# Output product of a slot-based expert layer: float32 in the two halves of TensorE's rows in place of float32r operands in two parts

## Chip, cores and metric

The kernel runs on one core of one Trainium2 chip. The metric is the device time of one execution in microseconds (us), lower is better. All times of instructions come from one profiled execution.

## Reference

An input of 8 x 2496 rows of 256 values goes through a two-dimensional Fourier transform, of which the real part is kept. The result `x` (19968 rows) passes a soft mixture of experts with 32 slots (8 experts of 4 slots):

```python
logits = x @ phi                                   # 19968 x 32
d = exp(logits - logits.max(0)); d /= d.sum(0)     # over rows
slot_out[e] = relu((d.T @ x)[e] @ w1[e]) @ w2[e]   # 32 x 256 in all
c = exp(logits - logits.max(1)); c /= c.sum(1)     # over slots
return c @ slot_out                                # 19968 x 256
```

The change concerns the last line: every row of the output is a sum of 32 products, float32.

## The kernel before

The 8 batches are worked on as four pairs p. For each pair the rows are loaded and folded (`part_a`), transformed and multiplied with phi in several small products (`part_z`, `part_t`, `part_b`, `part_c`), and the exponentials over rows give the slot inputs (`part_e`, `part_d`, `part_u`). `part_m`, `part_l` and `part_v` merge the pairs and run the two expert layers; their result is `so` in PSUM, one copy of the slots in each of four groups of 32 partitions. `part_r` sums the four groups with one product by the table `sel2` (tile `sorep`, L515), so that each group of 32 partitions holds the whole 32 x 256 `slot_out`, and writes it as the moving operand `rh`.

`part_s(p)` transposes the logits of a pair (tile `cT`, L534, three PSUM tiles), copies them to `c` with ScalarE (L539), and normalises them over the slots in two halves of 20 places: maximum on VectorE (L548), subtraction on GpSimd (L549), exponential on ScalarE (L550), sum and reciprocal on VectorE (L551 to L553), product on GpSimd (L554). A place is 128 rows of output with 32 weights each, so `c` is 128 partitions x 40 places x 32 slots.

The output is then made in 20 tiles (p, b): four pairs, five tiles each, eight places in a tile. Of each tile:

- `part_q` has split `c` in two parts, both float32r: ScalarE casts it (L560), and VectorE subtracts the cast from it (L561). The tile `hl` holds for each place 32 values of the first part and 32 of the second.
- `part_o` transposes two places at a time (four transposes, `lT`, L574), so that 128 partitions hold place, part and slot. ScalarE copies the four to `lTs` (L575).
- For each of the four couples i of places, two products (j = 0, 1) of 128 x 128 by 128 x 512 accumulate in one PSUM bank `po` (L581). `rh[0]` holds the cast of `slot_out` and `rh[1]` what the cast left over, each with zeros where a place meets the other's columns.
- ScalarE copies even i to the output tile and VectorE odd i (L585). SyncE writes the tile to memory when it is full (L590, L592).

PSUM banks: even i take turns on two (`ps`), odd i on three (`ps3`), and `lT` and `cT` share two (`p1`). Six output tiles can be in flight (`RING`), three `lTs` (`et`). The parts are written in the order of the string `ORDER`, and the framework's scheduler then sets the order of the instructions on each engine; every engine works in that order. The float32 products of the earlier stages give a `tile_position`, a place in the array: L246, L378, L477 and L497 use a quarter of its columns, L337 and L355 a half. L231, L281, L299, L300, L534 use the whole.

Of the kernel before, what the change touches and what calls it, by code (L numbers as in the profile page):

```python
# [5 lines left out]

F32 = mybir.dt.float32
F32R = mybir.dt.float32r
AF = mybir.ActivationFunctionType
ALU = mybir.AluOpType  # L10
AX = mybir.AxisListType
# [5 lines left out]
D = 256  # L17
NSLOT = 32
# [7 lines left out]
LA = 0  # L26
LD = '0 00 1 01 p 02 03 04 10 11 12 2 13 14 3'.split()
LT = 4
CT = ['sa', 'lt', 'lt', 'lt']
HT = ['se', 'zs']  # L30
RH = 0
LATE = 'zs'
SEB = 2
DE = 2
GP = 3
FIRST = [0, 1]
# [3 lines left out]
    "a00 z00 a01 z01 a02 z02 t00 a10 z10 b00 a11 z11 c00 c01 e00 e01 d00 a12 z12 t10 a20 z20 a21 z21 "  # L40
    "a22 z22 d01 b10 c10 e10 u00 a30 z30 d10 t20 c11 e11 b20 d11 c20 c21 a31 z31 "
    "e20 a32 z32 t30 e21 u10 b30 d20 c30 w00 d21 c31 u20 e30 e31 d30 d31 "
    "u30 m00 l00 s00 l10 q00 s10 v00 v10 r00 o00 q01 o01 q10 o02 o03 "
    "o04 o10 s20 q11 o11 q20 o12 o13 q21 o14 s30 o20 o21 q30 o22 o23 "
    "q31 o24 o30 o31 o32 o33 o34"
).split()


# [1 line left out]
def _tables():  # L50
    j = np.arange(128)
# [9 lines left out]
    c = np.arange(NKC)  # L61
# [7 lines left out]
    def block(t):  # L69
        return np.kron(eye, t)  # L70

    half = np.where(kc == 0, 0.5, 1.0)[:, None]
    ta = np.concatenate([cj[1:], co[:1]])
    g = np.arange(128) // NSLOT
    s = np.arange(128) % NSLOT
# [24 lines left out]
        ("psum", (g[:, None] // 2 * NSLOT + s[:, None]) == np.arange(64)),  # L100
        ("sel", np.arange(6)[:, None] + 6 * (np.arange(256) // 128) == np.tile(s, 2) // GS),
        ("sel2", s[:, None] == s[None]),
    ]
    out, where = [], {}
    for group in (zero, first, third, second, late):
        width = sum(t.shape[1] for _, t in group)
        arr = np.zeros((128, width), np.float32)
        o = 0
# [8 lines left out]
def _build(nc, tc, xh, phih, w1h, w2h, cins, where, out, out0):  # L117
    from contextlib import ExitStack, nullcontext

    v, sc, pe = nc.vector, nc.scalar, nc.tensor  # L120
    ctx = ExitStack()
    with ctx:
        cp = ctx.enter_context(tc.tile_pool(name="cp", bufs=1))
        sb = ctx.enter_context(tc.tile_pool(name="sb", bufs=1))
# [4 lines left out]
        def ring(name):  # L129
            return sb.tile([128, 8, D], F32, name=name, tag="ring", bufs=RING)  # L130
# [7 lines left out]
        def et(shape, name, dt=F32):  # L138
            return sb.tile(shape, dt, name=name, tag="et", bufs=3)

        def bufs_(tag):
            return {"zs": 2, "sa": 2, "se": SEB, "lt": LT}[tag]

        def bank(name, dt=F32):
            return pp.tile([128, 512], dt, name=name, tag="ps")
# [4 lines left out]
        def bank1(name, dt=F32):  # L150
            return p1.tile([128, 512], dt, name=name, tag="p1")
# [25 lines left out]
        def C(name):  # L177
            i, o, r, w = where[name]
            return cs[i][:r, o : o + w]

        ident = C("ident")
# [3 lines left out]
        ps = bank("psphi")  # L185
# [23 lines left out]
        zs, zt, o1, dpm, esb, dsb = {}, {}, {}, {}, {}, {}  # L209
# [217 lines left out]
        anchor = {}  # L427
# [41 lines left out]
        rh = []  # L469
# [34 lines left out]

        def part_r():
            so = sos_[0]
            for j in range(2):
                rh.append(sb.tile([128, 2, D], F32R, name=f"rh{j}", tag="d", bufs=2))
                nc.gpsimd.memset(rh[j].bitcast(F32), 0.0)
            v.tensor_copy(identr, ident)  # L510
            sos = sb.tile([128, D], F32, name="sos", tag="dpm", bufs=2)
            ps = bank("sorep")
            sc.copy(sos[:, :128], so[:, :128])
            v.tensor_copy(sos[:, 128:], so[:, 128:D])
            pe.matmul(ps[:, :D], C("sel2"), sos, start=True, stop=True)  # L515
            half = [slice(0, 64), slice(64, 128)]
            sc.copy(rh[0][half[0], 0, :], ps[half[0], :D])
            (v.tensor_copy if RH else sc.copy)(rh[0][half[1], 1, :], ps[half[1], :D])
            for k, r in enumerate(half):
                v.tensor_tensor(rh[1][r, k, :], ps[r, :D], rh[0][r, k, :].bitcast(F32), op=ALU.subtract)  # L520

        identr = sb.tile([128, 128], F32R, name="identr", tag="mex2", bufs=1)


        hl, cq = {}, {}

        def part_s(p):
            L = lt[p]
# [24 lines left out]
                v.reciprocal(m[:, 1], m[:, 1])  # L553
                e2.tensor_tensor(c, c, m[:, 1].unsqueeze(2).to_broadcast([128, 20, NSLOT]), op=ALU.mult)  # L554

        def part_q(p, i):
            c = cq[p][:, 20 * i : 20 * i + 20]
            e3 = nc.gpsimd if GP & 4 else v
            t = sb.tile([128, 20, 2, NSLOT], F32R, name=f"hl{p}_{i}", tag=HT[i], bufs=bufs_(HT[i]))
            sc.copy(t[:, :, 0], c)  # L560
            e3.tensor_tensor(t[:, :, 1], c, t[:, :, 0].bitcast(F32), op=ALU.subtract)  # L561
            hl[p, i] = t


        n_ev = [0]

        def part_o(p, b):
            ps = bank1(f"lT{p}_{b}", F32R)
            lT = et([128, 4, 128], f"lTs{p}_{b}", F32R)
            with tc.issue_after(anchor["v1"]) if LA and p == 0 else nullcontext():  # L570
              for i in range(4):
                k0 = 8 * b + 2 * i
                src = hl[p, k0 // 20][:, k0 % 20 : k0 % 20 + 2].rearrange("p k h s -> p (k h s)")
                pe.transpose(ps[:, i * 128 : i * 128 + 128], src, identr)  # L574
            sc.copy(lT, ps.rearrange("p (i n) -> p i n", i=4))  # L575
            ot = ring(f"o{p}_{b}")
            done = 0
            for i in range(4):
                po = (bank, bank3)[i % 2](f"po{p}_{b}_{i}")
                for j in range(2):  # L580
                    pe.matmul(  # L581
                        po, lT[:, i, :], rh[j].rearrange("p k d -> p (k d)"), start=j == 0, stop=j == 1,
                    )
                np_ = 64 if b == 4 and i == 3 else 128
                (v.tensor_copy if n_ev[0] % 2 else sc.copy)(  # L585
                    ot[:np_, 2 * i : 2 * i + 2, :].rearrange("p k d -> p (k d)"), po[:np_]
                )
                n_ev[0] += 1
                if b == 4 and i == 3:
                    nc.sync.dma_start(out0[p].rearrange("p (r d) -> p r d", d=D), ot[:64, 6:8])  # L590
                elif i == 3 or (b == 4 and i == 2) or ((p, b) == (0, 0) and i in FIRST):
                    nc.sync.dma_start(  # L592
                        out[p, :, (8 * b + done) * D : (8 * b + 2 * i + 2) * D].rearrange("p (r d) -> p r d", d=D),
                        ot[:, done : 2 * i + 2],
                    )
                    done = 2 * i + 2

        def after(f, *a):
            at_ = {0: None, 1: anchor.get("u"), 2: anchor.get("l")}[CAFTER]
            if at_ is None:  # L600
                return f(*a)
            with tc.issue_after(at_):
                return f(*a)
# [2 lines left out]
            "a": part_a, "z": part_z, "t": lambda p, _: part_t(p), "b": lambda p, _: part_b(p), "c": part_c,  # L606
            "e": part_e, "d": part_d, "u": lambda p, _: part_u(p), "w": lambda *_: load_w(),
            "m": lambda *_: part_m(), "l": lambda i, _: part_l(i), "v": lambda i, _: part_v(i),
            "r": lambda *_: part_r(), "s": lambda p, _: after(part_s, p), "q": lambda p, i: after(part_q, p, i), "o": part_o,
        }  # L610
        for what in ORDER:
            parts[what[0]](int(what[1]), int(what[2]))
# [50 lines left out]
```

## Time and profile before

| what | value |
|---|---|
| median of 3 runs | 196.1 us (195.84 to 196.13) |
| profiled execution | 195.98 us, span 194.2 us |
| TensorE busy | 170.9 us, 88% of the span |
| VectorE, ScalarE busy | 131.2 and 120.5 us |
| GpSimd busy | 24.6 us |
| written to memory | 20.45 MB |
| first product of the last stage | at 136.67 us |
| last copy of the last stage | at 184.83 us |

In the rows of the profile a group is given as line, engine, operation, out<-in, sizes and count, then busy us and mean ns of one, then the idle time ahead and what ended it. PE is TensorE's product, PEld its weight load, DVE VectorE, ACT ScalarE, POOL GpSimd, SPq the queue of SyncE. A piece of the chain of waits has start, length, engine and line.

### The profile page before, as it was taken

The numbers are of one execution on the slowest core, as the hardware profiler recorded it, in microseconds if no ns is written. First come the engines' busy times: TensorE is split into PE (matmuls) and PEld (weight loads), VectorE is DVE, ScalarE is ACT, GpSimd is POOL, SyncE is SP. The second block draws the span as 40 slices with busy tenths as digits, with TensorE's granted clock in tenths as the row PEclk, the third lists the DMA queues.
The fourth block names the chain that finished last, engine by engine and source line by source line (L and its number), as shares of the span: only waits on it lengthen the run. The fifth ranks groups of instructions, "written<-read, shape, count | busy, mean of one in ns | idle before, by whom it ended". The sixth has DMA issues, their size and how long they took to land.

```text
span 194.2 us, 4324 instructions
## 1 busy us (share of the span) xinstructions
PE 170.9 (88%) x1722; PEld 124.2 (64%) x1722; DVE 131.2 (68%) x238; ACT 120.5 (62%) x261; POOL 24.6 (13%) x27
## 2 busy tenths in 40 slices
PE   0489799899999989999998999999999999989900
PEld 0375496576776857577854877357788867768600
DVE  0599869999995971712456734994777888967600
ACT  2133686578954584775843827745868988997610
POOL 0000000000000000000000203576003157400000
PEclk9999999999999999999999999999999999999985
DMA  5999999999970699403940889970299999799996
GB/s 180 404 427 412 420 416 423 417 419 422 408 250 0 191 395 427 176 0 102 273 169 3 295 277 361 414 286 1 74 417 366 412 410 379 305 425 368 418 432 216
DMA packets 10707, 59.17 MB, mean 305 GB/s; under 512 B 1344, under 2 KB 1728, under 8 KB 5696
## 3 DMA queue, kind: packets, MB, share of 16 engines
q1 hardware_dynamic: 10688, 58.91, 77.1%
q8 instruction: 13, 0.21, 0.5%
q14 instruction: 6, 0.05, 0.1%
HBM read 38.46 MB, written 20.45 MB: 303 GB/s over the span
## 4 chain that ended last, share of the span: by engine, by line
PE 78%; DVE 7%; ACT 5%; DMA 2%; POOL 2%; issue 2%; SPq 0%; ACTq 0%; DVEq 0%; POOLq 0%
PE po L581 17%; PE pt L231 10%; PE z L246 8%; PE e L337 7%; PE d L355 5%; PE a L281 5%; PE u L378 4%; PE h L477 4%; PE so L497 4%; PE cT L534 3%; DMA x<-xh 2%; PE lp L299 2%; PE lm L300 2%; PE lT L574 2%; POOL c L549 2%; PE zt L267 2%
## 5 line engine op out<-in xcount | busy, mean ns | idle before, releaser
L581 PE MATMUL po<-rh,lTs 128*128 128x512 f32 x160 | 42.4, 405 | 1.5 <-ACT lTs L575 0.7
L581 PEld LDWEIGHTS po<-rh,lTs 128*128 128x128 f32 x160 | 28.1, 188 | 8.6 <-ACT o L585 1.8
L231 PE MATMUL pt<-cs,eo 128*128 128x128 f32 x160 | 25.7, 295 | 7.9 <-DVE eo L226 7.7
L585 DVE COPY o<-po 128x512 f32<-128x512 f32 (+1 forms) x40 | 26.9, 686 | 7.9 <-PE po L581 7.0
L232 ACT COPY et<-pt 128x512 f32<-128x512 f32 x40 | 22.8, 587 | 14.0 <-PE pt L231 13.9
L231 PEld LDWEIGHTS pt<-cs,eo 128*128 128x128 f32 x160 | 19.2, 150 | 14.6 <-DVE eo L226 7.7
L585 ACT COPY o<-po 128x512 f32<-128x512 f32 x40 | 23.2, 595 | 7.3 <-PE po L581 7.1
L224 DVE TENSOR_TENSOR x<-x 128x1024 f32<-128x1024 f32 x16 | 19.3, 1214 | 3.2 <-DMA x<-xh 3.2
L246 PE MATMUL z<-et,wphi 128*32 128x256 f32 (+1 forms) x288 | 16.8, 368 | 2.3 <-ACT et L232 2.3
L322 ACT ACTIVATE d<-lt,nm 120x128 f32<-120x128 f32 x44 | 13.7, 391 | 3.6 <-DVE nm L319 3.6
L549 POOL TENSOR_TENSOR c<-c,cm 128x640 f32<-128x640 f32 x8 | 11.8, 1487 | 27.1 <-DVE cm L548 26.0
L246 PEld LDWEIGHTS z<-et,wphi 128*32 128x32 f32 x288 | 8.1, 114 | 9.2 <-ACT et L232 3.8
L337 PE MATMUL e<-cs,dpm 120*64 120x120 f32 x176 | 13.9, 273 | 0.0
L226 DVE TENSOR_TENSOR eo<-x 128x512 f32<-128x512 f32 x20 | 13.7, 683 | 0.3
L227 DVE TENSOR_TENSOR eo<-x 128x512 f32<-128x512 f32 x20 | 13.6, 679 | 0.0
L337 PEld LDWEIGHTS e<-cs,dpm 120*64 120x64 f32 x176 | 11.4, 136 | 2.4 <-issue 1.8
L281 PE MATMUL a<-cs,zt 128*120 128x128 f32 x88 | 11.8, 279 | 1.0 <-DVE lt L304 0.9
L254 ACT COPY zs<-z 128x512 f32<-128x512 f32 (+1 forms) x12 | 6.2, 514 | 10.4 <-PE z L246 10.4
L554 POOL TENSOR_TENSOR c<-c,cm 128x640 f32<-128x640 f32 x8 | 11.0, 1391 | 10.0 <-DVE cm L553 5.5
L575 ACT CAST lTs<-lT 128x512 fp32r<-128x512 f32 x20 | 11.5, 599 | 0.9 <-PE lT L574 0.9
L281 PEld LDWEIGHTS a<-cs,zt 128*120 128x120 f32 x88 | 10.4, 183 | 2.1 <-DVE lt L304 1.1
L378 PE MATMUL u<-eo,ds 128*32 128x129 f32 x320 | 11.5, 275 | 0.1
(99 smaller groups left out, 242.5 us busy)
## 6 DMA issues: line engine op xcount, KB each, us to landing
x<-xh SPq DMA_DIRECT2D x16, 1024.0 KB, 11.9
out<-o SPq DMA_DIRECT2D x15, 1024.0 KB, 4.9
w<-w1h SPq DMA_DIRECT2D x6, 1024.0 KB, 8.4
w<-w2h SPq DMA_DIRECT2D x12, 512.0 KB, 6.2
x<-xh SPq DMA_DIRECT2D x4, 896.0 KB, 12.4
out<-o SPq DMA_DIRECT2D x4, 768.0 KB, 6.3
w<-w1h SPq DMA_DIRECT2D x4, 512.0 KB, 5.1
w<-w2h SPq DMA_DIRECT2D x2, 1024.0 KB, 7.0
```

Of the source, the lines that this page charges most:

```text
L224: v.tensor_tensor(x[:, 0:4], x[:, 0:4], x[:, 4:8], op=ALU.add)
L226: v.tensor_tensor(e[:, :, 0:128], x[:, 0:4, 0:128], x[:, 0:4, 128:256], op=ALU.add)
L231: pe.transpose(b[:, g * 128 : g * 128 + 128], e[:, g, k * 128 : k * 128 + 128], ident)
L232: sc.copy(tr[k][:, :, :, qi, :], b.rearrange("p (g h a) -> p g h a", g=4, h=2))
L246: pe.matmul(z[32 * g : 32 * g + 32, o : o + n], wphi[:, w, :], tr[k][:, g].rearrange("p h q a -> p (h q a)"), start=w != 0, stop=w != 1, t ...
L281: pe.matmul(ps[:120, i * 128 : i * 128 + 128], zt[p][:, GS * g : GS * g + GS].rearrange("p s h c -> p (s h c)"), C("wa"), start=True, stop ...
L322: sc.activation(d[:, g], L[:, g], AF.Exp, bias=nm[:, g : g + 1], scale=1.0)
L337: pe.matmul(ps[64 * k : 64 * k + 64, 120 * i : 120 * i + 120], dpm[p, hf][:, k, 3 * j + i, :], C(name), start=True, stop=True, tile_positi ...
L378: last = pe.matmul(ub[32 * g : 32 * g + 32, 0:129], dsb[p][:, k, c, :], e[:, 0:129] if k == 0 else e[:, 127:256], start=cc == 0, stop=cc == 9,
L549: e1.tensor_tensor(c, c, m[:, 0].unsqueeze(2).to_broadcast([128, 20, NSLOT]), op=ALU.subtract)
L581: pe.matmul(po, lT[:, i, :], rh[j].rearrange("p k d -> p (k d)"), start=j == 0, stop=j == 1,)
L585: (v.tensor_copy if n_ev[0] % 2 else sc.copy)(ot[:np_, 2 * i : 2 * i + 2, :].rearrange("p k d -> p (k d)"), po[:np_])
```

## The change

The two-part operands go. `part_q` with its cast and its subtraction is removed, and so are `identr`, `rh[1]` and the two memsets. `c` itself, in float32, is transposed: one transpose takes four places (128 partitions of place and slot), so a tile has two transposes instead of four, and `lTs` has 256 columns instead of 512.

A couple i of places then stands in 64 partitions: even i in 0 to 63, odd i in 64 to 127. Each couple takes one float32 product with 64 rows, 128 columns and 512 moving columns, at the place (0, 0) or (64, 0) of the array. `rh` is one float32 tile, 128 x 2 x 256: in each group of 32 partitions one of the two blocks of 256 columns holds `slot_out` and the other zeros. ScalarE writes the one block as the product of `sorep` with a column of the new table `turn`, VectorE the other. `turn` is 1 where the group number is even, in its first column, or odd, in its second. Two places that follow each other are issued together and then copied out, as before by ScalarE for even i and VectorE for odd i.

```diff
-            for j in range(2):
-                rh.append(sb.tile([128, 2, D], F32R, name=f"rh{j}", tag="d", bufs=2))
-                nc.gpsimd.memset(rh[j].bitcast(F32), 0.0)
-            v.tensor_copy(identr, ident)
+            rh.append(sb.tile([128, 2, D], F32, name="rh", tag="d", bufs=2))
...
-            sc.copy(rh[0][half[0], 0, :], ps[half[0], :D])
-            (v.tensor_copy if RH else sc.copy)(rh[0][half[1], 1, :], ps[half[1], :D])
-            for k, r in enumerate(half):
-                v.tensor_tensor(rh[1][r, k, :], ps[r, :D], rh[0][r, k, :].bitcast(F32), op=ALU.subtract)
+            sc.activation(rh[0][:, 0], ps[:, :D], AF.Copy, scale=C("turn")[:, 0:1])
+            v.tensor_scalar(rh[0][:, 1], ps[:, :D], C("turn")[:, 1:2], None, op0=ALU.mult)
...
-        def part_q(p, i):
-            c = cq[p][:, 20 * i : 20 * i + 20]
-            e3 = nc.gpsimd if GP & 4 else v
-            t = sb.tile([128, 20, 2, NSLOT], F32R, name=f"hl{p}_{i}", tag=HT[i], bufs=bufs_(HT[i]))
-            sc.copy(t[:, :, 0], c)
-            e3.tensor_tensor(t[:, :, 1], c, t[:, :, 0].bitcast(F32), op=ALU.subtract)
-            hl[p, i] = t
...
-              for i in range(4):
-                k0 = 8 * b + 2 * i
-                src = hl[p, k0 // 20][:, k0 % 20 : k0 % 20 + 2].rearrange("p k h s -> p (k h s)")
-                pe.transpose(ps[:, i * 128 : i * 128 + 128], src, identr)
-            sc.copy(lT, ps.rearrange("p (i n) -> p i n", i=4))
+            for t in range(2):
+                k0 = 8 * b + 4 * t
+                pe.transpose(
+                    ps[:, t * 128 : t * 128 + 128], cq[p][:, k0 : k0 + 4].rearrange("p k s -> p (k s)"), ident
+                )
+            sc.copy(lT, ps[:, :256].rearrange("p (i n) -> p i n", i=2))
...
             for i in range(4):
-                po = (bank, bank3)[i % 2](f"po{p}_{b}_{i}")
-                for j in range(2):
-                    pe.matmul(
-                        po, lT[:, i, :], rh[j].rearrange("p k d -> p (k d)"), start=j == 0, stop=j == 1,
-                    )
+                pos.append((bank, bank3)[i % 2](f"po{p}_{b}_{i}"))
+                rows = slice(64 * (i % 2), 64 * (i % 2) + 64)
+                pe.matmul(
+                    pos[i], lT[rows, i // 2], rh[0][rows].rearrange("p k d -> p (k d)"),
+                    start=True, stop=True, tile_position=(64 * (i % 2), 0),
+                )
+                if i % 2 == 0:
+                    continue
+                part_ev(p, b, i - 1, pos[i - 1], ot)
+                part_ev(p, b, i, pos[i], ot)
```

The scheduler's order changes with it. On TensorE, from the transposes of pair 1's first tile to those of pair 2's logits (in `po_2_1` the tile is b = 2 and the couple i = 1; the last number is the buffer's), there stands before:

```order
L574 MATMUL lT_0_1819<-identr,hl_0_1740 128x128 x4
L581 MATMUL po_2_3_1763<-rh_1671,lTs_2_1744 128x512
L581 MATMUL po_2_3_1763<-rh_1673,lTs_2_1744 128x512
L581 MATMUL po_2_0_1751<-rh_1671,lTs_2_1744 128x512
L581 MATMUL po_2_0_1751<-rh_1673,lTs_2_1744 128x512
L581 MATMUL po_3_1_1780<-rh_1671,lTs_3_1769 128x512
L581 MATMUL po_3_1_1780<-rh_1673,lTs_3_1769 128x512
L581 MATMUL po_2_2_1759<-rh_1671,lTs_2_1744 128x512
L581 MATMUL po_2_2_1759<-rh_1673,lTs_2_1744 128x512
L534 MATMUL cT_0_1845<-cs_70,lt_943 128x120 x4
```

And after, to the second group of those transposes:

```order
L555 MATMUL lT_0_1773<-cs_70,c_1568 128x128 x2
L565 MATMUL po_2_1_1723<-rh,lTs_2_1716 128x512
L565 MATMUL po_2_3_1729<-rh,lTs_2_1716 128x512
L565 MATMUL po_2_0_1721<-rh,lTs_2_1716 128x512
L565 MATMUL po_3_1_1742<-rh,lTs_3_1735 128x512
L565 MATMUL po_2_2_1727<-rh,lTs_2_1716 128x512
L525 MATMUL cT_0_1793<-cs_70,lt_942 128x120 x4
L565 MATMUL po_3_3_1748<-rh,lTs_3_1735 128x512
L565 MATMUL po_4_1_1761<-rh,lTs_4_1754 128x512
L565 MATMUL po_3_0_1740<-rh,lTs_3_1735 128x512
L565 MATMUL po_4_3_1767<-rh,lTs_4_1754 128x512
L565 MATMUL po_3_2_1746<-rh,lTs_3_1735 128x512
```

Couples with odd i, which are in the lower half of the rows now, stand two in a row at the head of both stretches, and each stretch has two even and three odd ones.

On ScalarE, around pair 2's exponentials (`c_1844` before, `c_1792` after, is pair 2's weights), there stands before:

```order
L539 COPY c_1844<-cT_2_1857 128x40x8
L585 COPY o_4_1800<-po_4_0_1801 128x512
L585 COPY o_4_1800<-po_4_2_1809 128x512
L575 COPY lTs_1_1882<-lT_1_1881 128x512
L575 COPY lTs_2_1910<-lT_2_1909 128x512
L585 COPY o_0_1826<-po_0_0_1827 128x512
L550 ACTIVATE c_1844<-c_1844 128x640
```

And after:

```order
L530 COPY c_1792<-cT_2_1805 128x40x8
L579 COPY o_4_1758<-po_4_0_1759 128x512
L541 ACTIVATE c_1792<-c_1792 128x640
L579 COPY o_4_1758<-po_4_2_1765 128x512
L558 COPY lTs_1_1827<-lT_1_1826 128x256
L558 COPY lTs_2_1846<-lT_2_1845 128x256
L541 ACTIVATE c_1792<-c_1792 128x640
L579 COPY o_0_1778<-po_0_0_1779 128x512
```

The first exponential has moved from behind five copies to behind one. Around the end of `so`, two of pair 0's five groups of `lT` have moved into the products of `so` (L497), and the other three stand between `so` and `sorep`; before, two stood between them, two behind `sorep` and one in the product.

## Prediction before the run

> **What bounds the kernel now.** I read the page's groups first, then the writer by stretches, then the chain of waits through the last stage. The groups show what the last stage is made of.
>
> ```profile
> span 194.2 us, 4324 instructions
> ...
> HBM read 38.46 MB, written 20.45 MB: 303 GB/s over the span
> ...
> L581 PE MATMUL po<-rh,lTs 128*128 128x512 f32 x160 | 42.4, 405 | 1.5 <-ACT lTs L575 0.7
> L581 PEld LDWEIGHTS po<-rh,lTs 128*128 128x128 f32 x160 | 28.1, 188 | 8.6 <-ACT o L585 1.8
> L585 DVE COPY o<-po 128x512 f32<-128x512 f32 (+1 forms) x40 | 26.9, 686 | 7.9 <-PE po L581 7.0
> ...
> L585 ACT COPY o<-po 128x512 f32<-128x512 f32 x40 | 23.2, 595 | 7.3 <-PE po L581 7.1
> ...
> L549 POOL TENSOR_TENSOR c<-c,cm 128x640 f32<-128x640 f32 x8 | 11.8, 1487 | 27.1 <-DVE cm L548 26.0
> ```
>
> The product (L581) is the largest group of the program. The same last stage also writes all 20.45 MB. The busy times by stretch say how close the writer is to its own limit; the last three columns are TensorE's clock, the share of the DMA engines, and GB/s.
>
> ```profile
> 138.00:166.00 28.00, 27.50 (x153) 21.79 (x152) 22.87 (x38) 23.24 (x44) 8.66 (x6) 1.00 0.91 365
> 166.00:186.00 20.00, 17.92 (x90) 13.83 (x89) 13.54 (x24) 15.06 (x28) 2.49 (x2) 1.00 0.96 389
> 186.00:192.00 6.00, 0.00 (x0) 0.00 (x0) 0.00 (x0) 0.00 (x0) 0.00 (x0) 0.65 1.01 387
> ```
>
> TensorE has nothing left after 186, and the writer works at 387 GB/s until 192. From 166 on it moves 389 and 387 GB/s, 26 us x 0.388 = 10.1 MB, which is pairs 2 and 3 (half of 20.45 MB). So pair 2's first output leaves at about 166, and from there the writer is the bound. Before that it is at 0.91, and it waits for the product. A slip of pair 2's first output therefore goes to the end one for one; TensorE's time in pairs 2 and 3 counts only if a tile of output takes it longer than the writer's 1.05 MB / 0.388 = 2.7 us.
>
> The chain from the expert sum `so` into the product, and the pieces of one kind in it (start, us, what):
>
> ```profile
> 134.31 0.49 PE lT L574 x4
> ...
> 134.82 0.95 ACT lTs L575 x2
> ...
> 136.16 0.38 ACT rh L518
> ...
> 136.67 2.56 PE po L581 x10
> 139.24 0.29 PE lT L574 x4
> 139.53 1.92 PE po L581 x8
> ...
> 143.64 0.41 PE cT L534 x4
> ...
> 146.37 0.72 PE cT L534 x7
> ```
>
> TensorE is on the chain almost without a gap: 0.24 a product (1.92 / 8), 0.29 for a tile's four float32r transposes, 0.41 + 0.72 for the eleven transposes of a pair's weights.
>
> **The price of a float32 place.** No place of 64 rows runs before. The nearest rows are float32 products alone in the whole array (lp), two side by side in halves of the columns (d), four in quarters (h). The first three rows are of the timeline and of the groups, the last four of the chain.
>
> ```profile
> 29.51 0.81 PE L299 MATMUL lp<-o,cs 120*120 120x384 f32 x2
> L355 PE MATMUL d<-e,cs 128*64 128x320 f32 x64 | 10.7, 443 | 0.5 <-ACT ds L361 0.5
> L477 PE MATMUL h<-w,sT 128*32 128x512 f32 x64 | 7.8, 596 | 0.0
> 29.67 0.65 PE lp L299 x2
> 32.99 0.54 PE lp L299 x2
> 111.12 2.27 PE d L355 x16
> 120.22 5.44 PE h L477 x48
> ```
>
> A float32 product is two instructions: 64 of d are 32 calls. Alone it takes 0.65 for 384 columns, so 0.65 x 512/384 = 0.87 for 512. Two side by side cost no more: 16 instructions of d take 2.27, eight rounds of 0.28, against 0.27 for one of that width alone (0.54 / 2). Four of 512 columns take 5.44 / 12 = 0.45 a round. I carry that over to halves of the rows: a slot of 0.87 holds one even and one odd place. The other end is no overlap, 0.87 a place (first rival). The Trainium skill (TensorE: Matmul & The Clock Gate, Part 3) gives 3.07x for four tiles of 32 rows; an estimate from that, 77% of full overlap, would make the slot 1.13 and the sum below 6.2 us longer. No run here shows a row tile.
>
> Changing between the whole array and places costs something too (chain):
>
> ```profile
> 50.31 0.44 PE pt L231 x4
> 50.74 0.55 PE e L337 x4
> 51.30 0.58 PE pt L231 x4
> 51.88 1.38 PE e L337 x20
> ```
>
> Four float32 transposes take 0.44 in line with their like, 0.11 each, and 0.58 between tiled products: 0.15 for a change there and back. A whole-array instruction also waits until both halves are empty, so a stretch of product between two of them costs as many slots as its fuller half.
>
> **The sum, up to pair 2's first output.** Even places stand in rows 0 to 63, odd ones in 64 to 127. In the new order of TensorE, part of which stands in the section on the change, the fuller half of each stretch up to the end of pair 1 holds 4, 3, 3, 2, 2, 1, 2, 2, 1, 2, 2 places: 24 slots where 20 would do. For pairs 2 and 3 it is 1, 2, 2, 3, 2, 2, 2, 8.
>
> - Before: 80 products x 0.24 = 19.2; eight groups of lT x 0.29 = 2.3; cT 2 x 1.13 = 2.3. Together 23.8.
> - After: 24 x 0.87 = 20.9; 14 lT x 0.11 = 1.5; cT 2.3; ten changes x 0.15 = 1.5. Together 26.2, so +2.4. Without the changes it is +0.9. If a place could not overtake one that waits for its own half, five stretches that open with two places of one half lose up to a slot each, +4.3. Against that, one of d's instructions starts ahead of an e instruction that the order has before it:
>
> ```profile
> 55.74 0.48 PE L355 MATMUL d<-e,cs 128*64 128x320 f32 x1
> 55.83 0.27 PE L337 MATMUL e<-cs,dpm 120*64 120x120 f32 x1
> ```
>
> - The way in. lT of tiles 0 and 1 now stands among the products of `so`, where TensorE is the chain: 4 x 0.11 + 0.15 = 0.6, which used to lie in the wait for `sos`. lT of tiles 2, 3 and 4 stands ahead of `sorep`, and tile 4 needs a bank of the two that ScalarE frees only after copying `sos` and tile 2.
>
> ```profile
> L515 PE MATMUL sorep<-sos,cs 128*128 128x256 f32 x2 | 0.7, 431 | 0.0
> L520 DVE TENSOR_TENSOR rh<-sorep,rh 64x256 fp32r<-64x256 f32 x2 | 0.8, 422 | 1.6 <-ACT rh L518 1.6
> L517 ACT CAST rh<-sorep 64x256 fp32r<-64x256 f32 x1 | 0.4, 370 | 0.0
> L514 DVE COPY sos<-so 128x128 f32<-128x128 f32 x1 | 0.3, 290 | 0.5 <-ACT sos L513 0.5
> L513 ACT COPY sos<-so 128x128 f32<-128x128 f32 x1 | 0.3, 266 | 1.1 <-PE so L497 1.1
> ```
>
>  Two tiles of lT (0.49 as before), ScalarE's copy of 256 columns (0.37, as L517's), and tile 4's 0.22 with two hand-overs put `sorep` about 1.4 after `so`. Before, it is sos, then sos on the other engine, 0.27 + 0.29 and hand-overs, 0.7. So +0.7. The new rh is one copy on ScalarE, then one on VectorE (they read one bank, as sos shows): 0.37 + 0.42 against 2 x 0.37, nothing. Way in: +1.3, bounds 0 and 1.7.
> - ScalarE's order. The second block of rows in the section on the change shows the first exponential of pair 2 moved ahead of four copies. It waits for VectorE's maximum and GpSimd's subtraction.
>
> ```profile
> L548 DVE TENSOR_REDUCE cm<-c 128x20 f32<-128x640 f32 x8 | 6.2, 810 | 1.7 <-ACT c L539 1.7
> ```
>
>  0.81 + 1.49 = 2.30, less one copy (0.59) in between now: ScalarE stands for 1.7; in pair 3 two copies are in between, 1.1. Behind it wait the copies out of the even places, which have two banks. Sum 2.8; it is nothing if TensorE is so far ahead that the banks are full anyway, so bounds 0 and 2.8. I take 2.8, since ScalarE's load of these ten tiles (20 x 0.595 for outputs alone) leaves little to catch up with.
> - Gone are ScalarE's and VectorE's steps of hl and half of every lTs copy. They are off the chain but for that wait; I count nothing for them in the sum; the most they could give is what the writer lacks in its first 28 us, 28 x (1 - 365/388) = 1.7, which the third rival takes.
>
> Slip: 2.4 + 1.3 + 2.8 = 6.5. After it a tile costs TensorE 2 x 0.87 + 0.22 + 0.15 = 2.1, less than the writer's 2.7, so the writer carries the slip to the end. The profiled execution took 195.98 (span 194.2, 1.8 around it), the median of the three runs is 196.1: the sum is 195.98 + 6.5 = **202.5 us**. Its own range: 195.98 + 0.9 + 1.3 = 198 with no wait on ScalarE and free changes; 195.98 + 6.5 + 4.3 + 1 = 208 without overtaking.
>
> **Rivals.**
> - *The halves do not run side by side.* 80 x 0.87 + 30 x 0.11 + 2.3 + 18 x 0.15 = 77.9 from 138.0 on: TensorE ends at 215.9. Then the last copy and landing, some 4.5, and the 4.0 that separate the writer's end at 192 from 195.98: **224**. For it: no row tile is in the trace. Against: column tiles overlap fully.
> - *The loads show.* If a half's next weights are loaded only once its product is done, each slot grows by two loads of 0.19 (L581's PEld row): 24 x 0.38 = 9.1, and a tile in pairs 2 and 3 takes 2.9 instead of 2.7, +2 in ten: **213.5**. Against: pt's transposes follow at 0.11. The Trainium skill (same title and part) states that a weight load overlaps products in flight only where the row groups differ. The rows of L581 show 28.1 us of loads under 42.4 of products on one row group, so the trace speaks against the rule for the whole array; no run shows it for halves.
> - *The other side: the writer hides it all.* If transposes slip between the halves at no cost, TensorE needs 20 slots in pairs 0 and 1, 17.4 + 1.5 + 2.3 = 21.2 instead of 23.8. With ScalarE and VectorE lighter, the writer could then be fed fully from its start: the 1.7 go, and the later start costs +1.3: **195.6**, from 194.3 with no later start to 196.0 at its upper bound. It decides where a tile in pairs 0 and 1 takes under 2.7 us, waits included; I have 2.6 without waits and 2.9 with them, so it is close by.
>
> **How the numbers follow.** The sum 0.73, no overlap 0.13, loads 0.05, writer 0.09. The likeliest gives 202.5. The range 195 to 208 takes in the sum's bounds and the writer's case; it leaves out the first two rivals, 0.18. Within 0.2% (0.4 us, about what a measurement of this kernel tells from none) I put 0.04 and faster 0.05, both from the writer's case, slower 0.91.
>
> **What would show it.** The group of po has 160 instructions again, of a mean near h's 596 ns, two at a time; if they start 0.43 apart one after another, the first rival is right. The writer's first stretch must fall below 365 GB/s, pair 2's first output must leave near 172, and ScalarE must show a wait on GpSimd of some 3 us ahead of L541. If pair 2 leaves by 166, the sum is wrong from its first line.

## The result and the profile after

| | before | after |
|---|---|---|
| median | 196.12 us (195.84 to 196.4) | 203.76 us (203.21 to 203.95) |
| ratio | | 1.0385 (95% interval 1.0363 to 1.0407) |
| profiled execution, its span | 195.98, 194.2 us | 203.76, 201.7 us |
| first product of the last stage | 136.67 us | 138.01 us |

The change costs 7.6 us, where 6.5 was forecast. Runs at a lower granted TensorE clock are left out everywhere; one of the two of experiment 1 was such a run (299.57 us at 0.736). First the groups of the page, in the order in which those of before were shown.

```profile
span 201.7 us, 4216 instructions
...
HBM read 38.46 MB, written 20.45 MB: 292 GB/s over the span
...
L565 PE MATMUL po<-rh,lTs 64*128 64x512 f32 x160 | 47.6, 617 | 1.7 <-DVE rh L513 1.1
L579 ACT COPY o<-po 128x512 f32<-128x512 f32 x40 | 23.4, 587 | 19.8 <-PE po L565 19.6
L565 PEld LDWEIGHTS po<-rh,lTs 64*128 64x128 f32 x160 | 17.9, 185 | 19.1 <-issue 8.8
```

The product has 160 instructions again, of 617 ns each, near the 596 ns of `h`. ScalarE now waits 19.6 us for the product ahead of its copies (7.1 before): TensorE is behind. The writer by stretches (last columns: TensorE's clock, share of the DMA engines, GB/s):

```profile
138.00:166.00 28.00, 27.37 (x111) 12.16 (x112) 17.74 (x29) 15.96 (x33) 5.75 (x5) 1.00 0.74 296
166.00:186.00 20.00, 20.00 (x79) 8.11 (x79) 13.14 (x23) 11.79 (x25) 4.27 (x4) 1.00 0.82 330
186.00:192.00 6.00, 6.00 (x24) 2.60 (x24) 3.78 (x6) 4.18 (x9) 0.00 (x0) 1.00 1.02 424
```

In the first 28 us it moves 296 GB/s instead of 365, and TensorE is busy for 27.4 of them (27.5 before, so its busy time does not tell the two apart). SyncE's queue shows when pair 2's first output is issued (start, us, queue, line), before:

```profile
166.22 0.33 SPq L592 DMA_DIRECT2D out<-o  x1
```

and after:

```profile
173.94 0.33 SPq L586 DMA_DIRECT2D out<-o  x1
```

That is 7.72 later, and the profiled execution is 7.78 longer (203.76 - 195.98). From the issue to the end it takes 29.76 before and 29.82 after: the slip goes to the end one for one. TensorE is busy until 193.3 now, yet from some 4 us behind that output on the writer is the bound in both kernels: its DMA engines are at 1.00 from 178 to 198 (402 GB/s), and before at 1.01 from 170 to 190 (404 GB/s). The chain from the way in to pair 2 says where the 7.7 come from (start, us, what; pieces in between left out):

```profile
120.41 5.44 PE h L475 x48
...
138.01 3.78 PE po L565 x15
...
142.15 2.77 PE po L565 x10
...
145.48 2.83 PE po L565 x10
148.33 0.59 ACT o L579
...
150.74 1.27 POOL c L540
152.03 0.74 ACT c L541
152.77 0.48 ACT o L579
153.29 2.25 PE po L565 x6
...
155.92 1.05 PE po L565 x2
...
157.34 1.91 PE po L565 x6
...
166.29 3.29 PE po L565 x7
...
185.94 7.32 PE po L565 x26
```

A stretch of four slots takes 3.78, of three 2.77 and 2.83, of two 1.91, of one 1.05. At 148.33 the chain leaves TensorE: a copy on ScalarE, GpSimd's subtraction, ScalarE's exponential, the next copy, and only then a product. At 166.29 two slots take 3.29 instead of 1.91. In this stretch stand the last places of pair 1 and the first of pair 2. What holds these is pair 3's first exponential, which ScalarE has ahead of its copies of `lT`:

```profile
166.56 0.74 ACT L541 ACTIVATE c<-c 128x640 f32<-128x640 f32 x1 [0.23 <-POOL c L540]
167.20 0.63 ACT L558 COPY lTs<-lT 128x256 f32<-128x256 f32 x2
```

The first of these copies ends at 167.56, and the first place that needs it starts at 167.61. Here ScalarE waits only 0.23 for GpSimd; the exponential itself takes more.

### The profile page after: what moved, and what is told of

It is laid out like the page before. It is cut to its first block, busy times and chain, and to the rows that moved or that the text cites. A ratio compares the mean times of both kernels' runs of the same rounds, so it can differ in the third digit from the quotient of the medians.

```text
span 201.7 us, 4216 instructions
## 1 busy us (share of the span) xinstructions
PE 178.7 (89%) x1682; PEld 110.1 (55%) x1682; DVE 126.0 (62%) x228; ACT 111.9 (55%) x252; POOL 20.8 (10%) x25
## 4 chain that ended last, share of the span: by engine, by line
PE 80%; DVE 6%; ACT 5%; DMA 2%; issue 1%; POOL 1%; SPq 0%; ACTq 0%; DVEq 0%
PE po L565 22%; PE pt L229 9%; PE z L244 8%; PE e L335 6%; PE d L353 5%; PE a L279 4%; PE u L376 4%; PE h L475 4%; PE so L495 3%; PE lT L555 3%; DMA x<-xh 2%; PE cT L525 2%; PE lp L297 2%; PE lm L298 2%; PE zt L265 2%; ACT et L230 2%
## 5 line engine op out<-in xcount | busy, mean ns | idle before, releaser
L565 PE MATMUL po<-rh,lTs 64*128 64x512 f32 x160 | 47.6, 617 | 1.7 <-DVE rh L513 1.1
L579 ACT COPY o<-po 128x512 f32<-128x512 f32 x40 | 23.4, 587 | 19.8 <-PE po L565 19.6
L565 PEld LDWEIGHTS po<-rh,lTs 64*128 64x128 f32 x160 | 17.9, 185 | 19.1 <-issue 8.8
L540 POOL TENSOR_TENSOR c<-c,cm 128x640 f32<-128x640 f32 x8 | 10.0, 1265 | 74.8 <-DVE cm L539 73.6
L353 PE MATMUL d<-e,cs 128*64 128x320 f32 x64 | 10.7, 443 | 0.5 <-ACT ds L359 0.5
L545 POOL TENSOR_TENSOR c<-c,cm 128x640 f32<-128x640 f32 x8 | 10.1, 1264 | 6.6 <-DVE cm L544 6.6
```

The costliest lines, as they stand in the source:

```text
L353: pe.matmul(ps[64 * h : 64 * h + 64, :320], C("wb")[:, 64 * k : 64 * k + 64], esb[p].rearrange("p g (s h c) -> p (g s) h c", h=2, c=NKC)[: ...
L565: pe.matmul(pos[i], lT[rows, i // 2], rh[0][rows].rearrange("p k d -> p (k d)"), start=True, stop=True, tile_position=(64 * (i % 2), 0),)
L579: (v.tensor_copy if n_ev[0] % 2 else sc.copy)(ot[:np_, 2 * i : 2 * i + 2, :].rearrange("p k d -> p (k d)"), po[:np_])
```

## Experiments

The theory: the slip is the sum of three things, stretches in which one half has more places than the other, ScalarE standing for GpSimd's subtraction, and the later way in. The main rivals: the halves do not run side by side, and the writer's feed depends on something else than pair 2's first output. `tc.issue_after(x)` in a diff keeps the scheduler from placing an instruction ahead of x. Each kernel is compared with the kernel before on the same chip, whose median was 196.4 to 196.5. That is some 0.4 us more than beside the changed kernel (196.12), so of what an edit takes out both figures are given: the difference of the medians, and the difference of the ratios times 196.3. They are good to about half a microsecond.

### 1. All products in one half

```diff
-                rows = slice(64 * (i % 2), 64 * (i % 2) + 64)
+                rows = slice(0, 64)
-                    start=True, stop=True, tile_position=(64 * (i % 2), 0),
+                    start=True, stop=True, tile_position=(0, 0),
```

The odd couples' own output is left out (they multiply the even couples' weights again); TensorE's order is that of after.

> The changed kernel with all 80 products in rows 0 to 63: the order of every instruction on TensorE is the same, only the place in the array is. The odd couples of places take the even couples' operands, so their output is left out. Theory: in the changed kernel the halves run side by side, and here they can't: 80 x 0.87 and the rest one after another, 222 to 226 us, with products that start 0.43 apart. Rival: side by side gave little (the Trainium skill's figure of 3.07 for four row tiles, or weight loads in the way), and one half costs less than 12 us more: under 216.

The profiled execution took 227.12 us, 1.1 above the theory's range and far from the rival's. The chain has the same stretches:

```profile
138.67 7.13 PE po L565 x16
...
146.17 4.49 PE po L565 x10
...
164.78 1.05 PE po L565 x2
```

Eight places take 7.13 in one half, 0.89 each, where after has 3.78; five places take 4.49, where after has 2.77 for two even and three odd. A single place takes 1.05 in both. So the halves run side by side at no visible cost, and a stretch costs what its fuller half costs. The rival without overlap, put at 224, describes this kernel and not the changed one.

### 2. Even and odd couples in turn

```diff
+                with tc.issue_after(anchor["po"]) if "po" in anchor else nullcontext():
+                    anchor["po"] = pe.matmul(
-                pe.matmul(
                     pos[i], lT[rows, i // 2], rh[0][rows].rearrange("p k d -> p (k d)"),
                     start=True, stop=True, tile_position=(64 * (i % 2), 0),
                 )
```

Each product is tied to the one before it, so that the order is even, odd, even, odd, tile by tile: 20 slots up to the end of pair 1 instead of 24.

> The changed kernel (203.8 us), with the 80 products tied to alternate between the halves (even, odd, even, odd, in the order of the tiles); nothing else is set. Theory: a stretch of product between two whole-array instructions costs as many slots of 0.87 as its fuller half, so pairs 0 and 1 need 20 slots instead of 24, and with the unpaired places 3.5 us go: 200.3 us, between 199 and 201.5. Rival: the unpaired places cost nothing, because the banks or the copies out set the pace anyway: 203 to 204.5.

198.48 us (198.29 to 198.57), ratio 1.0095 (1.007 to 1.012): 5.3 us of the 7.6 go (5.7 by the ratios), more than the slots alone and below the forecast range. The chain:

```profile
142.41 1.92 PE po L566 x8
...
153.07 2.23 PE po L566 x8
...
178.54 7.36 PE po L566 x32
```

A tile is one stretch of 1.92, and there is no piece of 3.29 any more; the slowest tiles take 2.23. The waits behind ScalarE have shrunk with the lost slots, so the two terms are not independent.

### 3. The exponentials of pairs 2 and 3 later on ScalarE

```diff
+                with tc.issue_after(anchor[{2: ("e100", "e102"), 3: ("e142", "e142")}[p][i]]) if p > 1 else nullcontext():
-                sc.activation(c, c, AF.Exp)
+                    sc.activation(c, c, AF.Exp)
```

(`e100` is the copy out of pair 1, tile 0, couple 0, and so on.) TensorE's order is that of after.

> The changed kernel with the four exponentials of pairs 2 and 3 put behind later copies on ScalarE (as many as stood there before the change); TensorE's order is the same. Theory: ScalarE's standing still for GpSimd holds the banks of the even places, some 3 us: 200.5 us, between 200 and 201.5. Rival: the weights of pairs 2 and 3 come later by as much and their transposes wait instead: 203 to 204.5.

201.3 us (200.93 to 201.55), ratio 1.0238 (1.0211 to 1.0266): 2.5 us go (2.9 by the ratios). The two places in the chain, where after has 153.29 for the first piece's start and 3.29 for the second piece:

```profile
152.03 2.38 PE po L566 x7
...
165.16 2.34 PE po L566 x7
```

So the stretches lose most of their wait (2.38 and 2.34 are still 0.45 above 1.92).

### 4. The way in

```diff
+            anchor["rep"] = pe.matmul(ps[:, :D], C("sel2"), sos, start=True, stop=True).ins
-            pe.matmul(ps[:, :D], C("sel2"), sos, start=True, stop=True)
...
+                with tc.issue_after(anchor["v1" if b < 2 else "rep"]) if p == 0 else nullcontext():
-                pe.transpose(
+                  pe.transpose(
```

Pair 0's `lT` of tiles 0 and 1 stand behind `so` (`v1` is its last product), those of tiles 2 to 4 behind `sorep`.

> The changed kernel with pair 0's transposes put back: tiles 0 and 1 behind the last product of the expert sum, tiles 2 to 4 behind the product that gathers the four groups. The order of everything after that is the same. Theory: the way in costs 1.3 us of the loss (0.6 for transposes in the chain, 0.7 for the bank that tile 4 waits for), and the slip goes to the end: 202.5 us, between 202.2 and 203. Rival: the way in is made up for later: 203.5 to 204.

203.28 us (202.93 to 204.02), ratio 1.0346 (1.0304 to 1.0388). The chain:

```profile
121.08 5.45 PE h L475 x48
...
136.98 0.37 ACT lTs L559
137.40 0.44 PE lT L556 x2
137.84 3.71 PE po L566 x15
```

From the start of `h` to the first product it now takes 16.76, against 17.60 in after and 16.45 before (136.67 less 120.22): 0.8 of the way in goes, and tile 4's transposes, which wait for a bank, keep 0.3. In the time 0.5 shows (0.8 by the ratios), between the theory's range and the rival's; its interval reaches the ratio of after, so the time alone does not show it, and the chain has to.

### 5. All three together

The edits of experiments 2, 3 and 4 in one kernel.

> The three edits of the first experiments together: products alternate, pair 0's transposes behind the expert sum, exponentials of pairs 2 and 3 behind later copies. Theory: the way in adds its 0.9 to what the alternation gave (198.5), but most of ScalarE's wait went with the alternation already, where three stretches are 0.3 longer than the rest: 197.0 us, between 196.5 and 197.6. Rival: the three are separate terms and add up, 198.5 - 0.9 - 2.5 = 195.1, faster than the kernel before.

196.8 us (196.25 to 197.58), ratio 1.0014 (0.9991 to 1.0038): level with the kernel before, and in the theory's range. Singly the edits gave 5.3, 2.5 and 0.5 us, 8.3 in all; together 7.0 (by the ratios 9.4 and 7.3). The chain now goes by pair 3's weights:

```profile
162.86 0.75 ACT c L542
...
166.26 1.27 POOL c L546
167.58 0.44 PE lT L557 x2
```

TensorE itself rests little: it works up to 167.14 and stands for 0.44 until pair 3's weights are there for the transposes at 167.58. What puts off pair 2's first output is VectorE. Pair 3's exponentials, which now come late, are followed by its two sums (L543), and the copies of that output's odd couples stand behind these:

```profile
163.63 1.54 DVE L543 TENSOR_REDUCE cm<-c 128x20 f32<-128x640 f32 x2 [0.53 <-ACT c L542]
166.17 1.22 DVE L582 COPY o<-po 128x512 f32<-128x512 f32 x2
```

The first copy of the last row ends at 166.80, and the output is issued at 166.86. The kernel before has a wait of this kind, which I had read over: its chain, too, comes to pair 2 by way of GpSimd.

```profile
160.79 3.68 POOL c L549 x2
164.49 0.22 ACT c L550
```

These are pair 3's subtractions and its second exponential; a copy of pair 2's first output stands behind them on ScalarE, ends at 166.19, and the output is issued at 166.22.

### 6. Fewer changes

Experiment 2 with the way in free, and `lT` of two tiles written together ahead of their products (`part_o` is split, and `T` writes the transposes; of the edit only the order is shown), so that there are half as many changes between places and the whole array:

```diff
-    "u30 m00 l00 s00 l10 s10 v00 v10 r00 o00 o01 o02 o03 "
-    "o04 o10 s20 o11 o12 o13 o14 s30 o20 o21 o22 o23 "
-    "o24 o30 o31 o32 o33 o34"
+    "u30 m00 l00 s00 l10 s10 v00 v10 r00 T00 T01 o00 T02 T03 o01 o02 T04 T10 o03 o04 "
+    "s20 T11 T12 o10 o11 T13 T14 o12 o13 s30 o14 T20 T21 o20 T22 T23 o21 o22 T24 T30 o23 o24 "
+    "T31 T32 o30 o31 T33 T34 o32 o33 o34"
```

> Products alternate, and the transposes stand in groups of two tiles written ahead of the products of the tile before, so that TensorE changes between the whole array and the halves about half as often; pair 0's third tile and later are transposed behind the first tile's products, so that nothing waits for a bank on the way in. Theory: up to pair 2's first output two changes of 0.35 go and the way in loses its 1.1: 197 us, between 196.3 and 197.7; the changes that go in pairs 2 and 3 are hidden by the writer. Rival: every change counts, nine of them by 0.35 and 1.1 more: 194.2, faster than before.

201.98 us (201.31 to 202.92), ratio 1.0273 (1.0232 to 1.0313): neither theory. The new order put the exponentials ahead of copies again:

```profile
152.00 0.74 ACT c L541
...
163.76 2.49 POOL c L540 x2
...
167.82 3.33 PE po L573 x8
```

So this kernel does not price the changes; it shows the wait on GpSimd's subtraction a second time, 3.33 for two slots.

### 7 and 8. More work for TensorE, behind and ahead of pair 2's first output

Experiment 2 with two idle transposes in some of the tiles (into the bank's unused columns, read by nobody), in the last eight tiles in experiment 7, and with `(1, 0) <= (p, b) < (2, 2)`, the seven tiles ahead of pair 2's third, in experiment 8:

```diff
+            if (p, b) > (2, 1):
+                for t in (2, 3):
+                    pe.transpose(
+                        ps[:, t * 128 : t * 128 + 128],
+                        cq[p][:, 8 * b + 4 * (t - 2) : 8 * b + 4 * (t - 2) + 4].rearrange("p k s -> p (k s)"), ident,
+                    )
```

Behind it:

> The alternating kernel (1.0095 of the kernel before) with two idle transposes more in each of the last eight tiles, into columns of the bank that nothing reads: 8 x 0.22 = 1.8 us more for TensorE after pair 2's first output. Theory: the writer is the bound there, a tile takes TensorE 2.5 instead of 2.3 against the writer's 2.6: less than 0.4 us more, 198.2 to 198.8 by a kernel before of 196.3. Rival: TensorE is the bound to the end: 1.8 more, 200.

198.0 us (197.39 to 199.39), ratio 1.008 (1.0052 to 1.0108); experiment 2 has 1.0095. TensorE's time there costs nothing, as forecast: the writer is the bound, its DMA engines at 1.01 from 166 to 186.

Ahead of it:

> The same two idle transposes more in the seven tiles whose transposes stand ahead of pair 2's first product (pair 1's, and pair 2's first two): 7 x 0.22 = 1.5 us. Theory: a slip of pair 2's first output goes to the end one for one, 1.5 more than the alternating kernel: 199.7 us, between 199.2 and 200.2. Rival: copies and the writer hide it here too: 198.2 to 198.8.

197.99 us (196.91 to 199.0), ratio 1.008 (1.0051 to 1.011). This theory fell, and the time is the rival's. In the chain pair 2's first output no longer hangs on TensorE:

```profile
159.66 0.83 DVE cm L539
160.56 2.50 POOL c L540 x2
...
164.61 2.17 PE po L572 x8
```

The product at 164.61 is released by a copy on ScalarE that stands behind pair 3's exponential and ends at 164.57; TensorE's own work ahead of it, with the idle transposes, ends at 164.56. Pair 2's first output is issued at 167.57, against 168.24 in experiment 2.

### 9 to 12. The logits of pairs 2 and 3 earlier

If ScalarE's waits and the late weights both come from the softmax of pairs 2 and 3, it might stand ahead of the product. In experiment 9 it does, with the edits of 2 and 4:

```diff
-    "... r00 o00 o01 o02 o03 "
-    "o04 o10 s20 o11 o12 o13 o14 s30 o20 ..."
+    "... r00 s20 o00 o01 s30 o02 o03 "
+    "o04 o10 o11 o12 o13 o14 o20 ..."
```

> The couples alternate, pair 0's transposes stand behind sorep as in the last combination, and the transposes and softmax of the logits of pairs 2 and 3 are written ahead of the product instead of inside it, so that no copy out of a couple waits for GpSimd and TensorE has all weights by the time it needs them. The price is the eleven transposes of pair 2 and part of pair 3's, which now stand between so and the first product (some 1 to 2 us later start). Theory: with nothing left that starves it, the writer is the bound from its first output on, so the time is its first issue plus 20.45 MB / 0.388 = 52.7 plus 2.9 for the last landing and what lies around the span: first issue near 140.5, 196.2 us (195.5 to 197). Rival: the moment of pair 2's first output decides alone, as in the prediction; it would leave at 163 and the time would be 193.

Experiment 10 is the same with `o00 s20 o01 o02 s30 o03`:

> As the one before, but the logits of pair 2 are written behind the first tile of outputs and those of pair 3 behind the third, so that fewer transposes stand ahead of the first product and more between the first tiles. Theory (writer the bound from its first output): first issue near 139.8, 195.5 us (194.8 to 196.5), 0.5 to 1 faster than the other variant. Rival (pair 2's first output alone decides): both variants within 0.3 of each other, near 193. A third way: the exponentials that still stand between the copies of the first three tiles stall them again, 197 to 198.

Experiment 11 is the changed kernel with 9's new order of parts alone:

> The changed kernel with only one thing altered: the logits of pairs 2 and 3 are written ahead of the product and behind its first two tiles. Two couples of one half still stand together in some stretches: 24 slots again up to pair 2's first output. If the slots, the changes and ScalarE's waits are separate terms, ScalarE's 3.2 and the two changes of the cT groups go and the later start costs up to 1.5: 203.8 - 3.2 - 0.7 + 1.5 = 201.4 at the worst; with the transposes of pair 2 out of the product's path as well (2 x 1.1, now ahead of it) 198 to 199.5. I expect 199 (197.5 to 200.5). Rival: without the waits the order of the couples costs nothing, since the copies then take each couple as it comes: within 0.5 of the kernel that also alternates them.

Experiment 12 is the kernel before with the same move:

> The kernel before (float32r in two parts) with only the same move of the logits of pairs 2 and 3. It tells whether what the move gives belongs to the halves or to any kernel of this form. Theory: there no copy stood behind a wait for GpSimd and the writer lacked only 1.7 us of its limit; the later start takes back what a steadier feed gives: 196.5 (195.5 to 197.5), the same as before within 0.5%. Rival: the transposes inside the product held the kernel before up as well, and it gains as much as the changed one, 194.

| experiment | median, us | ratio (95% interval) |
|---|---|---|
| 9, halves in turn, way in, logits ahead | 201.58 | 1.0246 (1.0223 to 1.027) |
| 10, the same, logits behind tiles 0 and 2 | 200.88 | 1.023 (1.0207 to 1.0254) |
| 11, after, logits ahead | 201.84 | 1.0255 (1.0231 to 1.0279) |
| 12, before, logits ahead | 201.6 | 1.0253 (1.0227 to 1.0278) |

All four theories missed, and the kernel before loses 5 us by the move. Of the rivals one came out in its number, that of experiment 11: it is within 0.3 us of experiment 9, so that with the logits ahead the order of the couples and the way in are worth nothing. Its reason did not, since waits stand in both. The writer by stretches in experiment 9:

```profile
138.00:166.00 28.00, 26.06 (x111) 10.82 (x111) 19.36 (x36) 17.62 (x37) 9.69 (x8) 0.94 0.71 284
166.00:186.00 20.00, 20.00 (x90) 7.54 (x89) 12.83 (x19) 13.14 (x27) 0.00 (x0) 1.00 1.01 401
```

and its chain through the first tiles:

```profile
143.75 0.95 POOL c L545
144.97 2.50 POOL c L540 x2
...
148.14 0.57 ACT o L581
148.76 3.40 PE po L567 x8
```

The softmax of two pairs now stands in the first tiles, and the copies wait there. The writer has no backlog yet to live on: it starves at its start, runs at its limit from 166 at the latest, and does not make the gap good. I had taken its first output for the moment that decides; it is the last output before which it stood idle.

That can be put in one sum for all kernels: issue of that output, plus what is left to write from there at 0.39 MB/us (the 387 to 389 GB/s of the kernel before), plus 3.6. The 0.39 is a mean and not the most that the writer does: after moves 424 GB/s from 186 to 192. The remainders are 10.22 MB from pair 2's first tile, 9.17 from its second, 15.34 from pair 1's first, 17.30 and 18.35 from pair 0's fourth and third.

| kernel | output that decides, issued | sum, us | profiled execution, us |
|---|---|---|---|
| before | pair 2's first, 166.22 | 166.22 + 26.2 + 3.6 = 196.0 | 195.98 |
| after | pair 2's first, 173.94 | 203.7 | 203.76 |
| 3 | pair 2's first, 171.85 | 201.7 | 201.34 |
| 4 | pair 2's first, 173.69 | 203.5 | 203.34 |
| 5 | pair 2's first, 166.86 | 196.7 | 196.71 |
| 6 | pair 2's second, 174.78 | 201.9 | 201.99 |
| 2 | pair 1's first, 155.94 | 155.94 + 39.3 + 3.6 = 198.8 | 198.29 |
| 7 | pair 1's first, 155.45 | 198.4 | 197.89 |
| 8 | pair 1's first, 155.20 | 198.1 | 198.13 |
| 9 | pair 0's third, 150.75 | 150.75 + 47.1 + 3.6 = 201.4 | 201.58 |
| 10 | pair 0's fourth, 151.13 | 151.13 + 44.4 + 3.6 = 199.1 | 199.08 |
| 12 | pair 0's fourth, 152.53 | 200.5 | 200.52 |

The output is the one for which the sum is largest (in experiment 5 pair 1's second, issued at 156.54, gives 196.8, as much). The 3.6 is fitted to these runs, so the table describes them and has not been tried on a further kernel. It agrees with experiment 8: what decides there is pair 1's first output, issued at 155.20, which the idle transposes, in tiles from pair 1 on, did not put off (155.94 in experiment 2). Experiment 11 fits less well (200.3 by its best output, 201.05 measured), and experiment 1 is bound by TensorE. For the kernel before, the first output of all, issued at 138.73, gives 138.73 + 52.4 + 3.6 = 194.7: by this sum no faster product behind the same start could win more than 1.3 us. The prediction's 0.91 for the first stretch hides that, since it takes in the start; from 142 to 166 the DMA engines of the kernel before are at 0.97.

## Why the prediction was right

The forecast of 202.5 us was right in sign and in its main mechanism, the slots of the halves and the slip of pair 2's first output, and 1.3 us short (203.76). That it came so near is in part luck: one term has its size for another reason, and two omissions work against each other. Its steps:

- *The slot holds an even and an odd place: right.* Stretches of one, two and three slots take 1.05, 1.92 and 2.77, steps of 0.87 and 0.85 against 0.87 forecast; eight slots at the end take 7.32, 0.92 each. Experiment 1 shows that this is overlap. The estimate from the Trainium skill (TensorE: Matmul & The Clock Gate, Part 3; 3.07x for four tiles of 32 rows) would have made a slot 1.13; for two halves the measurement is full overlap, and it decides.
- *Loads hidden: right.* They take 185 ns each, and a second place in the same half costs 0.89 (experiment 1), not 0.87 + 0.19 or more.
- *A stretch costs its fuller half: right,* 24 slots for 20. Experiment 2 removes the four, 3.5 us at 0.87, and gains 5.3, since waits go with them.
- *Overtaking, the bound of +4.3: it takes place.* In the second stretch the first two places of the order are both odd ones. Two places start at once even so, at 142.08 and 142.10, and the next two at 143.05, so the first even one has gone ahead of the second odd one; where a half is free TensorE does not keep to the order, as the section on the kernel before says of every engine.

```profile
142.08 0.71 PE L565 MATMUL po<-rh,lTs 64*128 64x512 f32 x2
```

- *A change there and back, 0.15: mis-sized.* In experiment 2 a tile with its own transposes takes 1.92 + 0.37 = 2.29, one of the last four without them 7.36 / 4 = 1.84. Of the 0.45, 0.22 are the transposes themselves: 0.23 a change. Ten of them make +0.8.
- *The way in, +1.3: 1.15,* by the chains from the start of `h`. Experiment 4 takes 0.8 of it out of the chain.
- *ScalarE standing for GpSimd, 2.8: right in size, half right in kind.* Experiment 3 takes 2.5 out and leaves 0.9 in the two stretches (2.38 and 2.34 against 1.92). But ScalarE stands for GpSimd only 1.20 and 0.23 us ahead of the two first exponentials, not 1.7 and 1.1, in part since the subtraction takes 1.27 there and not the mean of 1.49. What the term leaves out is the exponential itself, 0.74, which now stands ahead of copies that TensorE waits for (152.77 and 167.20 above). The sign I named, a wait of some 3 us on ScalarE ahead of L541, was a poor one: over the whole run such a wait stands in both kernels (`c` L550 waited 3.2 us before, `c` L541 2.8 after), and from 138 to 186 it is 0.9 and 1.4. What changed is what is queued behind it.
- *The sum: 6.5 forecast, 7.7 measured.* From the first product to the issue of pair 2's first output it is 29.55 before and 35.93 after, 6.4 where 5.2 was forecast. I stopped the count of TensorE's work at the end of pair 1 in both kernels. Before, TensorE has by then begun 96 products and ten groups of `lT`, 16 and 2 more than I counted: 16 x 0.24 + 2 x 0.29 = 4.4. After, two stretches and two `lT` stand behind my sum until pair 2's first tile is through: 1.05 + 1.91 + 2 x 0.37 = 3.7. That is -0.7. What the counted work leaves of the time is 29.55 - 23.8 - 4.4 = 1.35 before and 35.93 - 26.2 - 2.8 - 3.7 = 3.23 after, both put at nothing: +1.9. Before, the output hung on a copy behind pair 3's exponentials (experiment 5), and not on TensorE, as the prediction has it. After, the dearer changes are a part of the 3.23; a split to the tenth is not to be had from these runs.
- *One for one to the end: right here,* 29.76 and 29.82 from that issue to the end. As a rule it was too narrow: it holds while pair 2's first output is the last for which the writer waits, and experiments 2 and 6 to 12 have another.
- *The rivals.* No overlap and visible loads are refuted by experiment 1 (the loads' sum, 202.5 + 9.1 + 2, is 213.6 and not 213.5). That the writer hides it all did not come true for this kernel, but an edited one comes near it: with the couples in turn, the exponentials late and the way in free the change is worth nothing either way (experiment 5, 1.0014). By the traces the writer and pair 3's softmax ahead of pair 2's first copies set the time of both kernels then, and TensorE does not; that a kernel without this softmax in the way would be faster is not shown, and experiments 9 to 12, which moved it, were slower. No version here beats the kernel before.

## What to carry to other kernels

Two tiles in two halves of the array's rows gave their full gain here only where the order on TensorE alternates between them: read the order for stretches, count the fuller half of each, and add a change for each whole-array instruction in between. An engine that copies results out should have nothing in its queue that waits for a slower engine. Behind a writer near its limit, look for the last output for which it stands idle; work for TensorE behind that point was free here (experiment 7), and work moved ahead of it, as the logits, was paid for (experiments 9 to 12).

## What the runs showed of the hardware

GpSimd's subtraction of 128 x 640 has a mean of 1265 ns after and 1487 ns before, the same instruction. The shortest, the median and the longest of the eight (ns), after and before:

```profile
L540 POOL TENSOR_TENSOR c<-c,cm x8: 1262/1264/1268, 119.7 to 166.5; 128x640 f32<-128x640 f32 x8
L549 POOL TENSOR_TENSOR c<-c,cm x8: 1264/1267/2445, 119.5 to 163.2; 128x640 f32<-128x640 f32 x8
```

So the mean misleads. Before, six of the eight take as long as after, and two make the difference: 1.86 us at 129.44, and 2.45 us at 160.79, the one in the chain of experiment 5. Beside both stands one of VectorE's `hl` subtractions, which the change removes. But one stands beside the subtraction at 125.36 too (0.73 us of it), which takes 1.27, and in experiment 12 beside the one at 138.38 (1.05 us), which takes 1.26. Standing beside it is thus not enough to lengthen it, and why the two are long stays open.
